# Gated linear attention and a routed expert layer on one core: steps moved between the places of a slot

## The chip, the cores and the metric

The kernel runs on one core of one Trainium2 chip. A core has five engines that each run their own instructions in order and wait for one another through semaphores: TensorE (PE in the profile; its weight loads are a row of their own, PEld), VectorE (DVE), ScalarE (ACT), GpSimd (POOL) and SyncE (SP, which issues most transfers). The metric is the device time of one execution in microseconds; lower is better.

## The reference

Four sequences of 768 tokens with 8 heads of 48 go through a gated linear attention; its output, 3072 tokens of 384 numbers, goes through a layer of 8 experts, of which each token uses one.

```python
for t in range(S):                        # attention: S = 768, per sequence and head
    state = alpha[:, :, t, :, None] * state + np.einsum('bhd,bhe->bhde', k[:, :, t], v[:, :, t])
    y[:, :, t] = np.einsum('bhd,bhde->bhe', q[:, :, t], state)
...
for s in range(S):                        # experts: x is the attention's output
    fresh_e = int(np.argmax(logits[b, s]))
    if s == 0 or local_gate[b, s] < 0.5:
        e = fresh_e
    else:
        e = prev_e if prev_e >= 0 else fresh_e
    prev_e = e
    ...
    h = np.maximum(x[b, s] @ w1[e], 0.0)  # 384 -> 1024
    out[b, s] = p[e] * (h @ w2[e])        # 1024 -> 384
```

`logits` is the token times `w_gate`, `p` its softmax, and `local_gate` a sigmoid of the token times `w_local`. Which expert a token uses can depend on the tokens before it, so it is known only once the attention has reached it.

## The kernel before

**Attention in slots.** The 3072 tokens are 24 blocks of 128, taken in turn from the four sequences. The main loop has 26 slots `i`. In slot `i` stand, in program order: GpSimd's `one_a(i+2)`, which sets one column of ones in the loaded decay factors `a`; `scan2(i+1)` (VectorE's backward scan `sf`, then GpSimd's product of it with `k`, both in the tile `x`); `flush()`; `kt(i)` (TensorE transposes `k` into `kp`, ScalarE copies that to `kk`); `copies(i-1)` and `state(i-1)` (ScalarE copies the state to `sb`, VectorE makes the next one); `pm(i)` (TensorE's products `pe`, masked by VectorE to `pq`); three prepared steps from the list `made`; the first place; `scan1(i+2)` (VectorE's scan `A` and a reciprocal, GpSimd's product of `A` with `q`); loads of block `i+3`; `xt(i-2)` (transposes `xp` for the routing); `ym(i-1)` (TensorE's output products `y`, from `pq` and from `sb`; ScalarE copies it to `XR` and sends it to `xd` in memory); the weights' step; the second place; `um(i)` (TensorE's products `up`, which VectorE adds into the state `st`; in slots 0 to 3 GpSimd first clears that state); the third place. From `pinned[0] = True` on, each engine keeps this order.

**Places.** A place is one call of `other()` (lines 622 to 636). It first runs `flush()`, which issues the VectorE steps put off in the list `later`; then it takes one step of each routing that is under way; and then, while `work[0]` is empty, two products of zeros on TensorE (`dense(DN)`, lines 293 to 295: 128x256 into `h2`, whose result nobody reads). Once `work[0]` is set it takes steps of the early experts instead, one for each place, in the second and third places only as long as blocks come in (`other(i >= NB)`), and no zeros.

**Routing.** After every four blocks `route(g)` is put on the list `steps` in slot 4g+5, ahead of its second place. It is a generator: what stands between two `yield` is done in one place. Its chain is `lg` (logits), `lt`, `kr` (VectorE, seven small steps), an empty place, `rp`, `em`, `rb`, `oi`, `ex`, `pw`, `ps` (seven or eight small VectorE steps), `vo` and `on` over four places (in the last routing one), and `lp`, which VectorE adds into the lists `acc`: 16 places, in the last routing 13. All its results on TensorE (`lg`, `lt`, `rp`, `rb`, `pw`, `lp`) use one PSUM buffer, the tag `rt`.

**Early experts.** The third routing (`g = 2`) ends by making the first lists `idx` and setting `work[0] = early()`. This generator gathers the rows of expert 0 (two indirect transfers on GpSimd's queue, one a place), waits four places, transposes them (`trans`, tiles `tp`, `xh`, `xl`; `tp` shares the PSUM tag `tr` with `kp` and `xp`), and then multiplies: a piece of `gemm1` is nine products into `h` with ScalarE's `hh` and VectorE's `hl` behind it, a piece of `gemm2` six products into `yp`. Three jobs run this way (256 rows of expert 0, 256 and 224 of expert 1); what is left of the eight experts follows behind the loop as a dense stretch of products.

**Weights.** `Weights.steps()` (lines 145 to 160) brings in one expert in seven steps: a load of the raw tile on SP's queue some steps ahead, ScalarE's rounding copy (`w1h`, `w2h`), and a subtraction for the rest (`w1l`, `w2l`), which for the early experts is put off through `later` and runs on VectorE at the next `flush()`. Expert 0 takes one step a slot in slots 5 to 11, ahead of the second place (lines 717 to 721); expert 1's seven steps are taken between the pieces of the first job's `gemm2`.

**The start.** Ahead of the loop GpSimd clears the tiles `vt`, `sb` and `oh`, sets the constants `one`, `m5`, `c0`, `c1` and `trif`, and then `one_a(0)`; TensorE runs 32 products of zeros. `made` holds twelve prepared steps, three a slot, from `fill` over `acc`, `off`, `ioa` and `iob` to `vals`.

Of the kernel before, what the change touches and what calls it, by code (L numbers as in the profile page):

```python
# [66 lines left out]
def gla_moe(ctx, tc, akq, vw, vn, wg, w1, w2, cst, tok, out):  # L67
# [188 lines left out]
    with ExitStack() as ac, ExitStack() as aa:  # L256
# [16 lines left out]
        for j in range(2):  # L273
            sb = ap.tile([R, 2, 2, CW], F32, bufs=1, name=f"sb{j}")
            g_.memset(sb[0:64], 0.0)
            g_.memset(sb[64:112, :, 1, :], 0.0)
            SBs.append(sb)
            oh = ap.tile([128, E, G + 1], F32, bufs=1, name=f"oh{j}")
            g_.memset(oh, 0.0)
            OHs.append(oh)  # L280
# [38 lines left out]
        def scan1(i):  # L319

            d = blk[i]
            x, a = d["x"], d["a"]
            A = ap.tile([R, SW], F32, tag="A", bufs=3, name=f"A_{i}")
            v_.tensor_tensor_scan(A, a[:, 0:SW], z1, 0.0, ALU.mult, ALU.add)
            d["end"] = A[:, 2 * C + 1:SW:2 * (C + 1)]
            v_.reciprocal(z2[0:R, 2 * C + 1:SW:2 * (C + 1)], d["end"])
            q2 = x[:, BW:].rearrange("p (s t) -> p s t", t=C)
            g_.tensor_tensor(q2, q2, A.rearrange("p (s t) -> p s t", t=C + 1)[:, :, 1:], ALU.mult)
            d["k"] = x[:, 0:BW].rearrange("p (h t) -> p h t", h=HP)
            d["q"] = x[:, BW:2 * BW].rearrange("p (h t) -> p h t", h=HP)  # L330

# [100 lines left out]
        def route(g):  # L432
# [36 lines left out]
            yield  # L469
# [66 lines left out]
            if end:  # L536
                v_.tensor_tensor(on, iob.unsqueeze(1).broadcast_to([128, n, TS]),
                                 rr.unsqueeze(2).broadcast_to([128, n, TS]), ALU.is_equal)
            else:
                for j in range(n):  # L540
                    s_.activation(on[:, j], iob, AF.Abs, bias=rr[:, j:j + 1], scale=-1.0)
                    s_.activation(on[:, j], on[:, j], AF.Relu, bias=one[:, 0:1], scale=-float(TS))
                    if j < n - 1:
                        yield
# [17 lines left out]
        def early():  # L562
# [10 lines left out]
            for _ in range(4):  # L573
                yield False
# [47 lines left out]
        def other(pieces=True):  # L622

            flush()
            for r in list(steps):
                if next(r, 0) == 0:
                    steps.remove(r)
            if work[0] is None:
                if DN:
                    dense(DN)  # L630
            else:
                if last and drained[0]:
                    last[0].ht, last[0].yt = HL, YL
                for done in work[0] if pieces else ():
                    if done or steps or not drained[0]:
                        break

# [9 lines left out]
        g_.memset(one, 1.0)  # L647
        g_.memset(m5, 1.0)
        g_.memset(m5[:, :, 0], 0.0)
        for e in range(E):  # L650
            g_.memset(c0[:, e:e + 1], float(e * RS - 1))
            g_.memset(c1[:, e:e + 1], float(e * RS - 1 + (C1 if e in EARLY else 0)))
        g_.tensor_copy(trif, cc("tri"))
        g_.memset(trif[0:64, 64:128], 1.0)
        g_.memset(trif[64:128, 0:64], 0.0)
# [4 lines left out]
        made = [  # L660
            lambda: g_.memset(fill, 0.0),
# [14 lines left out]
            lambda: g_.tensor_copy(vals[:, :, 2], tk[:, 1:2 * NB:2]),  # L676
        ]
        one_a(0)
        scan1(0)
        scan2(0)  # L680
        one_a(1)
        scan1(1)
        wsteps = iter(())
        for i in range(NB + 2):
# [14 lines left out]
            for _ in range(min(3, len(made))):  # L699
# [20 lines left out]
            elif i > W0 + 2:  # L720
                next(wsteps, None)
            if i == T1:
                begin(EARLY[1], v_)
            other()
            if i < NB:
                um(i)
# [214 lines left out]
```

## Time and profile before

| | |
|---|---|
| time, median of 3 runs | 482.89 us (481.34 to 493.2) |
| profiled execution | 484.0 us, of which the span is 482.2 |
| instructions | 10873 |
| mean granted TensorE clock | 0.961 |
| products of zeros (`h<-dz`) | 142, 35.0 us busy |
| routing's gathers and stores of rows | 32 and 32, about 1.0 us of GpSimd each |
| bytes moved | 66.01 MB, mean 137 GB/s |

A busy TensorE need not be at its peak, since products are pipelined; `TENSOR_TENSOR_SCAN` is VectorE's running sum along a row. In a timeline row stand start and duration in us, engine, line, operation, `out<-in` by the program's names, the shape, and in brackets how long the engine was idle just before and what ended that. Since one helper records every operation, all have line 81; the tile's name tells them apart. Consecutive instructions overlap by some tens of ns, so that the distance of two starts is a better price than a duration.

### The profile page before, as it was taken

The page shows a single profiled execution, that of the slowest core. Times are in us where ns is not written, and L with a number is a line of the kernel's source. Part 1 is how long each engine was busy: PE and PEld are TensorE (multiplying, and loading weights), DVE is VectorE, ACT ScalarE, POOL GpSimd, SP SyncE. Part 2 cuts the span into 40 slices and gives each one's busy share as a digit, 9 for nine tenths or more (in the row PEclk, how much of TensorE's full clock was granted, in tenths as well). Part 3 has the DMA queues.
Part 4 walks back from the last instruction along what each step waited for, and adds up shares of the span by engine and source line. Part 5 has one row for each costly group of instructions (what it writes and reads, how often), then busy time and mean ns, then how long its engine had stood idle before and what let it go on. Part 6 is the DMA issues. An engine that isn't in the chain of part 4 may idle for free.

```text
span 482.2 us, 10873 instructions
## 1 busy us (share of the span) xinstructions
PE 437.9 (91%) x4443; PEld 391.5 (81%) x4443; DVE 257.3 (53%) x485; ACT 194.1 (40%) x390; POOL 186.7 (39%) x207
## 2 busy tenths in 40 slices
PE   5999898999997978698989999999999999999990
PEld 5777776878875877597878998998989989989990
DVE  4778999898997235722274445244254252342310
ACT  1345656565756436321354324335144233242210
POOL 6654326364556000261053642724732503504201
PEclk9799999999998899888899999999999999999997
DMA  8789767596661102660075554444351542531100
GB/s 217 199 260 252 222 187 201 164 292 167 189 208 50 51 17 71 180 186 27 1 224 188 134 181 138 124 131 123 114 175 57 158 130 65 174 98 39 50 3 27
DMA packets 26710, 66.01 MB, mean 137 GB/s; under 512 B 4384, under 2 KB 10677, under 8 KB 26658
## 3 DMA queue, kind: packets, MB, share of 16 engines
q1 hardware_dynamic: 18672, 49.65, 36.3%
q0 software_dynamic: 3840, 10.62, 6.9%
q10 hardware_dynamic: 4146, 5.03, 3.1%
q8 instruction: 35, 0.57, 0.5%
q14 instruction: 17, 0.14, 0.1%
HBM read 55.84 MB, written 10.62 MB: 138 GB/s over the span
## 4 chain that ended last, share of the span: by engine, by line
PE 53%; issue 11%; DVE 9%; ACT 3%; POOL 2%; POOLq 0%; DVEq 0%; ACTq 0%
PE h L81 24%; PE yp L81 20%; PE y L81 3%; PE tp L81 2%; DVE A L81 2%; POOL out L81 1%; PE up L81 1%; DVE st L81 1%; DVE sf L81 1%; DVE pq L81 1%; ACT hh L81 1%; POOL w1l_0b L81 1%; PE pe L81 1%; DVE xl L81 1%; PE lp L81 1%
## 5 line engine op out<-in xcount | busy, mean ns | idle before, releaser
L81 DVE SCALAR_TENSOR_TENSOR hl<-h,hh 128x480 fp32r<-128x480 f32 (+2 forms) x80 | 43.9, 556 | 77.2 <-ACT hh L81 76.9
L81 ACT ACTIVATE hh<-h 128x480 fp32r<-128x480 f32 (+2 forms) x80 | 38.7, 490 | 82.4 <-PE h L81 82.3
L81 POOL DMA_INDIRECT out<-yo,idx x32 | 32.5, 1017 | 80.5 <-DVE yo L81 78.0
L81 POOL DMA_INDIRECT xg<-xd,idx x32 | 32.6, 1018 | 61.0 <-PE tp L81 52.9
L81 DVE TENSOR_SCALAR yo<-yp,acc 128x384 f32<-128x384 f32 (+1 forms) x32 | 19.6, 616 | 61.1 <-PE yp L81 61.0
L81 POOL TENSOR_TENSOR x<-x,sf 112x512 f32<-112x512 f32 x24 | 29.0, 1209 | 42.5 <-DVE sf L81 42.5
L81 POOL TENSOR_TENSOR x<-x,A 112x512 f32<-112x512 f32 x24 | 31.8, 1327 | 29.0 <-DVE A L81 6.6
L81 DVE TENSOR_TENSOR_SCAN A<-a,z 112x520 f32<-112x520 f32 x24 | 34.5, 1437 | 5.6 <-POOL a L81 5.6
L81 PE MATMUL h<-dz 128*128 128x256 f32 x142 | 35.0, 354 | 2.1 <-DVE z L81 2.1
L81 DVE TENSOR_TENSOR_SCAN sf<-a,z 112x520 f32<-112x520 f32 x24 | 33.8, 1408 | 0.1
L81 ACT COPY sb<-st 48x384 f32<-48x384 f32 x48 | 24.5, 510 | 11.5 <-DVE st L81 10.9
L81 PEld LDWEIGHTS h<-dz 128*128 128x128 f32 x142 | 23.8, 224 | 6.5 <-DVE z L81 2.1
L81 PEld LDWEIGHTS y<-vt,pq 64*64 64x64 f32 x768 | 24.9, 138 | 4.0 <-issue 3.8
L81 PE MATMUL y<-vt,pq 64*64 64x48 f32 x768 | 27.9, 224 | 0.0
L81 PE MATMUL y<-sb,x 112*64 112x96 f32 x384 | 21.8, 258 | 4.3 <-ACT sb L81 4.2
L81 PE MATMUL up<-vt,kk 128*48 128x96 f32 (+1 forms) x384 | 23.1, 267 | 0.0
L81 PEld LDWEIGHTS y<-sb,x 112*64 112x64 f32 x384 | 17.2, 140 | 6.2 <-ACT sb L81 5.2
L81 PEld LDWEIGHTS up<-vt,kk 128*48 128x48 f32 (+1 forms) x384 | 18.3, 140 | 3.4 <-issue 1.0
L81 ACT COPY kk<-kp 128x448 f32<-128x448 f32 x24 | 12.8, 531 | 20.7 <-PE kp L81 20.6
L81 PE MATMUL h<-xh,w1h_1a 128*128 128x256 f32 (+1 forms) x48 | 16.4, 342 | 3.9 <-DVE hl L81 2.7
L81 ACT COPY XR<-y 128x384 f32<-128x384 f32 x24 | 11.5, 479 | 20.1 <-PE y L81 20.1
L81 ACT CAST xh<-tp 128x384 fp32r<-128x384 f32 (+1 forms) x32 | 14.0, 462 | 13.9 <-PE tp L81 13.6
(247 smaller groups left out, 1234.8 us busy)
## 6 DMA issues: line engine op xcount, KB each, us to landing
x<-akq SPq DMA_DIRECT2D x24, 448.0 KB, 5.6
a<-akq SPq DMA_DIRECT2D x24, 227.9 KB, 4.5
vt<-vn SPq DMA_DIRECT2D x24, 192.0 KB, 2.7
xd<-XR ACTq DMA_DIRECT2D x24, 192.0 KB, 4.8
rw_0a<-w SPq DMA_DIRECT2D x3, 512.0 KB, 4.9
rw_0a<-w SPq DMA_DIRECT2D x4, 384.0 KB, 4.2
rw_1a<-w SPq DMA_DIRECT2D x3, 512.0 KB, 5.9
rw_1a<-w SPq DMA_DIRECT2D x4, 384.0 KB, 3.5
```

Of the source, the lines that this page charges most:

```text
L81: r = f(*a, **k)
```

## The change

Four parts are changed at once.

- The start: the clearing of the second `sb`, of `oh`, and the constants `one`, `m5` and `trif` go from the start to the head of `made`. `c0` is no longer written by eight small GpSimd steps but computed from `ioa` by two VectorE steps at the end of `made`, and `c1` by a copy of it and two small steps. A slot takes five prepared steps instead of three. The product of `A` with `q` for block 0 (`scale_q(0)`) goes behind that of `sf` with `k`.
- The weights' step of slots 5 to 11 goes behind the second place and ahead of `um(i)`, so that its put-off subtraction runs in the third place, behind the addition into `st`.
- The routing loses its empty place, and `on` takes two places instead of four: 13 places, in the last routing 12. `early()` waits two places instead of four.
- Zeros are also issued while `work[0]` is set, as long as no job has begun its first `gemm1` (`last` is empty), in each place in which no transposes or products of the early experts are issued.

```diff
@@ -272,12 +272,11 @@
             VTs.append(vt)
         for j in range(2):
             sb = ap.tile([R, 2, 2, CW], F32, bufs=1, name=f"sb{j}")
-            g_.memset(sb[0:64], 0.0)
-            g_.memset(sb[64:112, :, 1, :], 0.0)
+            if j == 0:
+                g_.memset(sb[0:64], 0.0)
+                g_.memset(sb[64:112, :, 1, :], 0.0)
             SBs.append(sb)
-            oh = ap.tile([128, E, G + 1], F32, bufs=1, name=f"oh{j}")
-            g_.memset(oh, 0.0)
-            OHs.append(oh)
+            OHs.append(ap.tile([128, E, G + 1], F32, bufs=1, name=f"oh{j}"))
 
         st = {"c": c0}
         sts = [ap.tile([R, 3, HP, D], F32, tag="st", bufs=G + 1, name=f"st_{i}") for i in range(G)]
@@ -324,10 +323,15 @@
             v_.tensor_tensor_scan(A, a[:, 0:SW], z1, 0.0, ALU.mult, ALU.add)
             d["end"] = A[:, 2 * C + 1:SW:2 * (C + 1)]
             v_.reciprocal(z2[0:R, 2 * C + 1:SW:2 * (C + 1)], d["end"])
-            q2 = x[:, BW:].rearrange("p (s t) -> p s t", t=C)
-            g_.tensor_tensor(q2, q2, A.rearrange("p (s t) -> p s t", t=C + 1)[:, :, 1:], ALU.mult)
+            d["A"] = A
+            if i:
+                scale_q(i)
             d["k"] = x[:, 0:BW].rearrange("p (h t) -> p h t", h=HP)
             d["q"] = x[:, BW:2 * BW].rearrange("p (h t) -> p h t", h=HP)
+
+        def scale_q(i):
+            q2 = blk[i]["x"][:, BW:].rearrange("p (s t) -> p s t", t=C)
+            g_.tensor_tensor(q2, q2, blk[i].pop("A").rearrange("p (s t) -> p s t", t=C + 1)[:, :, 1:], ALU.mult)
 
         def one_a(i):
             a = blk[i]["a"]
@@ -466,7 +470,6 @@
             v_.scalar_tensor_tensor(m2, kr[:, 1, :, 0], 16.0, m2, ALU.mult, ALU.add)
             v_.tensor_tensor(kr[:, 0], ge, m2.unsqueeze(2).broadcast_to([128, n, 8]), ALU.is_equal)
             yield
-            yield
 
             rp = pp.tile([8 * n, 2, 128], F32, tag=RT, name=f"rp_{g}")
             for j in range(2):
@@ -540,7 +543,7 @@
                 for j in range(n):
                     s_.activation(on[:, j], iob, AF.Abs, bias=rr[:, j:j + 1], scale=-1.0)
                     s_.activation(on[:, j], on[:, j], AF.Relu, bias=one[:, 0:1], scale=-float(TS))
-                    if j < n - 1:
+                    if j == 1:
                         yield
             yield
 
@@ -570,8 +573,8 @@
                 j.load_list(0)
             for _ in jobs[0].gather():
                 yield False
-            for _ in range(4):
-                yield False
+            yield False
+            yield False
             for _ in jobs[0].trans():
                 yield True
             for n, j in enumerate(jobs):
@@ -625,15 +628,15 @@
             for r in list(steps):
                 if next(r, 0) == 0:
                     steps.remove(r)
-            if work[0] is None:
-                if DN:
-                    dense(DN)
-            else:
+            done = False
+            if work[0] is not None:
                 if last and drained[0]:
                     last[0].ht, last[0].yt = HL, YL
                 for done in work[0] if pieces else ():
                     if done or steps or not drained[0]:
                         break
+            if not done and not drained[0] and (work[0] is None or not last):
+                dense(DN)
 
         work, drained = [None], [False]
         for i in range(3):
@@ -644,20 +647,21 @@
                 nc.scalar.dma_start(cs, cst)
                 nc.scalar.dma_start(tk, tok)
                 nc.scalar.dma_start(wgs, wg[:, :, 0:32])
-        g_.memset(one, 1.0)
-        g_.memset(m5, 1.0)
-        g_.memset(m5[:, :, 0], 0.0)
-        for e in range(E):
-            g_.memset(c0[:, e:e + 1], float(e * RS - 1))
-            g_.memset(c1[:, e:e + 1], float(e * RS - 1 + (C1 if e in EARLY else 0)))
-        g_.tensor_copy(trif, cc("tri"))
-        g_.memset(trif[0:64, 64:128], 1.0)
-        g_.memset(trif[64:128, 0:64], 0.0)
         nc.scalar.dma_start(xd[0:1], z2[127:128, 0:DM])
         first_v(0)
         pinned[0] = True
         dense(DN0)
         made = [
+            lambda: g_.memset(SBs[1][0:64], 0.0),
+            lambda: g_.memset(SBs[1][64:112, :, 1, :], 0.0),
+            lambda: g_.memset(one, 1.0),
+            lambda: g_.memset(OHs[0], 0.0),
+            lambda: g_.memset(OHs[1], 0.0),
+            lambda: g_.memset(m5, 1.0),
+            lambda: g_.memset(m5[:, :, 0], 0.0),
+            lambda: g_.tensor_copy(trif, cc("tri")),
+            lambda: g_.memset(trif[0:64, 64:128], 1.0),
+            lambda: g_.memset(trif[64:128, 0:64], 0.0),
             lambda: g_.memset(fill, 0.0),
             lambda: g_.tensor_copy(fill.bitcast(I32)[:, 1:2], tk[0:SL, 2 * NB:]),
             lambda: g_.memset(acc, 0.0),
@@ -674,10 +678,16 @@
                                      tk[:, 0:2 * NB].rearrange("p (b j t) -> p t j b", b=G, t=2)[:, 0],
                                      -float(SENT), None, ALU.add),
             lambda: g_.tensor_copy(vals[:, :, 2], tk[:, 1:2 * NB:2]),
+            lambda: v_.tensor_scalar(c0, ioa[:, :, 0], WH, float(TS), ALU.subtract, ALU.mult),
+            lambda: v_.tensor_scalar(c0, c0, -1.0, None, ALU.add),
+            lambda: g_.tensor_copy(c1, c0),
+        ] + [
+            lambda e=e: g_.memset(c1[:, e:e + 1], float(e * RS - 1 + C1)) for e in EARLY
         ]
         one_a(0)
         scan1(0)
         scan2(0)
+        scale_q(0)
         one_a(1)
         scan1(1)
         wsteps = iter(())
@@ -696,7 +706,7 @@
                 pm(i)
             if i > NB:
                 drained[0] = True
-            for _ in range(min(3, len(made))):
+            for _ in range(min(5, len(made))):
                 made.pop(0)()
             other(i >= NB)
             if i + 2 < NB:
@@ -717,11 +727,11 @@
             if i == W0:
                 begin(EARLY[0], v_)
                 wsteps = EW[EARLY[0]].steps()
-            elif i > W0 + 2:
-                next(wsteps, None)
             if i == T1:
                 begin(EARLY[1], v_)
             other()
+            if i > W0 + 2:
+                next(wsteps, None)
             if i < NB:
                 um(i)
             other()
```

## The prediction

> **What bounds the kernel now.** I read the page first (engines, the 40 slices), then the windows view cut at the starts of the slots, then the timeline and the waits inside the slots that the change touches.
>
> ```profile
> PE 437.9 (91%) x4443; PEld 391.5 (81%) x4443; DVE 257.3 (53%) x485; ACT 194.1 (40%) x390; POOL 186.7 (39%) x207
> ...
> PEclk9799999999998899888899999999999999999997
> ```
>
> TensorE is busy for 91% of the span and at full clock in most slices, so only three things can go: its idle time, its time at a lower clock, and multiplications of zeros. Where those lie, the windows view tells. I cut it at the transposes `kp` of slots 0, 5, 12, 17, 21 and 23, at the last `lg`, and behind it. Columns: length, then busy time and instructions of TensorE, its weight load, VectorE, ScalarE and GpSimd, then the granted clock, the DMA share and GB/s.
>
> ```profile
> 11.25:40.63 29.38, 27.02 (x492) 22.60 (x493) 23.25 (x32) 12.23 (x25) 15.89 (x28) 0.89 0.85 240
> 40.63:88.96 48.33, 43.41 (x833) 36.27 (x832) 43.43 (x82) 29.74 (x66) 21.51 (x24) 0.96 0.68 196
> 88.96:119.94 30.98, 30.20 (x591) 25.48 (x590) 28.27 (x62) 18.64 (x45) 14.28 (x15) 1.00 0.77 226
> 119.94:142.53 22.59, 21.77 (x462) 18.20 (x461) 21.66 (x45) 15.17 (x37) 13.18 (x15) 1.00 0.73 214
> 142.53:163.21 20.68, 16.81 (x256) 13.82 (x257) 12.24 (x31) 10.14 (x26) 9.40 (x8) 0.83 0.19 54
> 163.21:180.97 17.76, 15.12 (x218) 13.22 (x216) 6.14 (x23) 7.70 (x19) 0.83 (x1) 1.00 0.07 24
> 180.97:203.94 22.97, 16.82 (x122) 14.60 (x121) 16.00 (x42) 11.08 (x24) 3.14 (x3) 0.96 0.44 127
> ...
> 262.00:420.00 158.00, 158.00 (x848) 146.29 (x847) 62.72 (x94) 56.92 (x90) 67.27 (x46) 1.00 0.43 129
> ```
>
> Slots 5 to 11 (second row) leave 4.9 us idle on TensorE and as much on VectorE: each waits for the other in turns. Slots 12 to 16 are bound by TensorE, with 0.8 us idle. From 142.5 to 203.9 TensorE idles 3.9, 2.6 and 6.2 us, and the clock drops. From 262 us on it is always busy; nothing there is touched, so what the change gains before stays gained.
>
> **The change part by part.** Costs are taken against the profiled execution: 484.0 us, of which 482.2 are the span. The median of the three runs is 482.89, 1.1 us less.
>
> *(a) GpSimd's constants and the start.* The first scan waits for `one_a(0)` on GpSimd, behind its constants.
>
> ```profile
> 3.34 1.20 POOL L81 MEMSET sb<- 64x768 f32 x2
> ...
> 6.20 0.11 POOL L81 MEMSET a<- 112x4 f32 x1
> 6.34 1.24 DVE L81 TENSOR_TENSOR_SCAN A<-a,z 112x520 f32<-112x520 f32 x1 [4.23 <-POOL a L81]
> ...
> 7.67 1.18 POOL L81 TENSOR_TENSOR x<-x,A 112x512 f32<-112x512 f32 x1 [1.36 <-DVE A L81]
> ...
> 7.83 2.11 DVE L81 TENSOR_TENSOR_SCAN sf<-a,z 112x520 f32<-112x520 f32 x1
> ...
> 11.28 1.24 DVE L81 TENSOR_TENSOR_SCAN A<-a,z 112x520 f32<-112x520 f32 x1 [1.33 <-POOL a L81]
> ...
> 36.56 0.56 DVE L81 TENSOR_TENSOR st<-up,st 112x384 f32<-112x384 f32 x1 [1.54 <-POOL st L81]
> ```
> ```profile
> cs<-cst ACTq DMA_DIRECT2D x1, 224.5 KB, 4.5
> ```
>
> What stands from 3.34 to 6.20 on GpSimd, 2.9 us, leaves the start. Then the load of `a` is late next: its landing has no row; `cs`, as large and issued at the same time (0.7 us), took 4.5, so about 5.2. The scan starts at 5.35 instead of 6.34. With the product for `q` moved back, the scan `sf` no longer runs beside it and takes 1.22 (row under (b)) instead of 2.11; but that product, 1.18, now stands between `k` and `one_a(1)`. The second scan: 5.35 + 1.24 for `A` + 0.25 to `sf` (as from 7.58 to 7.83) + 1.22 + 1.18 for each product + 0.23 for `one_a(1)` and two hand-overs = 10.65, against 11.28: -0.6 (bounds -1.0, and 0 if `a` lands only at 6.2). The 2.9 us come back on GpSimd in slots 0 and 1, all other prepared steps slide back by two slots, and three VectorE steps (`ioa`, `iob`) meet in slot 3. In slots 0 to 3 the step `st` waits for GpSimd (last row), so this is not free; but GpSimd waits for the scan `A` there too, which covers most. I take a fifth of 2.9, +0.6 (bounds 0 and +2.9). Sum of (a): 0.0.
>
> *(b) Weights' step behind the second place, slots 5 to 11.* ScalarE's rounding copy and VectorE's subtraction are the same instructions; the three loads of a step stay behind the same loads on SP's queue, as nothing else is issued there in between.
>
> ```profile
> DVE w1l_0a L81 <- ACT w1h_0a L81: 2.2, 3, 1.2
> DVE w2l_0a L81 <- ACT w2h_0a L81: 0.4, 1, 0.4
> ...
> DVE w2l_0a L81 <- ACT w2h_0a L81: 2.0, 1, 2.0
> ```
> ```profile
> 53.68 1.88 DVE L81 TENSOR_TENSOR w1l_0a<-rw_0a,w1h_0a 128x1024 fp32r<-128x1024 f32 x1 [0.31 <-ACT w1h_0a L81]
> 55.47 0.55 DVE L81 TENSOR_TENSOR st<-up,st 112x384 f32<-112x384 f32 x1
> 55.94 1.22 DVE L81 TENSOR_TENSOR_SCAN sf<-a,z 112x520 f32<-112x520 f32 x1
> ```
>
> VectorE waits 4.6 us in all for the rounding copies; the addition into the state `st`, ready since `up`, and the copies and products behind it wait along. After, `st` goes first: 0.47 us of each wait (55.47 to 55.94) is filled, some 1.6 over the four waits in slots 5 to 8, and 1.0 of the long one in slot 11, where the routing's steps stand ahead too. I take -2.6 (bounds 0, and -4.6 if all waits go). ScalarE's copy now stands behind the second place's small copies and just ahead of the next slot's `kk`; its idle time covers that, at 29.74 busy of 48.33.
>
> *(c) Routing in 13 places instead of 16 (the last in 12 instead of 13).* No instruction goes. But a routing starts every 12 places, in a slot's second place. Now the last step of one (`lp`, and VectorE's addition into `acc`) and the first of the next (`lg`) fall into the same place, and `lp` and `lg` share the one buffer `rt`. So TensorE stands at `lg` until `acc` is read, and `acc` stands behind the scan `A`. Behind `lg` are zeros and `up`, and for `up` wait `st` and the next scan. Before, slot 14 shows the same wait at `rp`, a place later and behind `up`:
>
> ```profile
> 98.60 1.36 PE L81 MATMUL lg<-xx,wgs 128*32 128x128 f32 x24
> ...
> 105.46 1.13 PE L81 MATMUL lp<-vo,on 128*128 128x96 f32 x8
> 106.37 0.48 PE L81 MATMUL h<-dz 128*128 128x256 f32 x2
> 106.78 0.88 PE L81 MATMUL up<-vt,kk 128*48 128x96 f32 x16
> 108.19 0.39 PE L81 MATMUL rp<-cs,kr 128*32 128x128 f32 x2 [0.53 <-DVE acc L81]
> ```
> ```profile
> 106.55 1.23 DVE L81 TENSOR_TENSOR_SCAN A<-a,z 112x520 f32<-112x520 f32 x1
> 107.82 0.18 DVE L81 RECIPROCAL z<-A 112x4 f32<-112x4 f32 x1
> 107.91 0.23 DVE L81 TENSOR_TENSOR acc<-acc,lp 128x96 f32<-128x96 f32 x1
> 108.06 0.55 DVE L81 TENSOR_TENSOR st<-up,st 112x384 f32<-112x384 f32 x1
> ```
>
> `lp` makes way at 106.37, `acc` is done at 108.14: 1.77 us idle, less the 0.53 that `rp` waits no more, is 1.2 a slot. Slots 9, 13 and 17 together: +3.6. Bounds: 0, if `acc` comes early, and +2.6 each, if VectorE is the bound: then it idles from 108.14 over `lg` (1.36), zeros (0.41, from 106.37 to 106.78) and `up` (0.88), that is +7.9. I take TensorE's value, since these slots are bound by it.
>
> *(d) Zeros up to the first early multiplication.* `early` is begun one slot sooner and has two steps less ahead of its first product, and takes two steps a slot: its first product moves from slot 22's third place to slot 20's. Zeros end with slot 18's first place now; after, they stand in five more: slot 18's other two, slot 19's first two, slot 20's first. That is 10 products more, 0.205 us each (106.37 to 106.78 for two), 2.1 us. VectorE is busy 21.66 of 22.59 us in slots 17 to 20 and hides a third: +1.5 (bounds 0 and +2.1). The two gathers of the first job are issued on GpSimd one slot sooner, between the same products for `k` and `q`; GpSimd, busy 13.18 of 22.59 us there, covers them, and without that the next `k` would come later by their issue.
>
> *(e) Four pieces of the first products two slots earlier.* They lengthen slots 20 to 24 by what they take, since TensorE has little idle time there, and leave the last routing. In it three of the seven weight steps, of this size, are then gone too, and one place:
>
> ```profile
> L81 DVE TENSOR_TENSOR w1l_1a<-rw_1a,w1h_1a 128x1024 fp32r<-128x1024 f32 x3 | 3.7, 1223 | 1.0 <-ACT w1h_1a L81 1.0
> ```
>
> The pieces move, their time stays; what can go is the 6.2 us that TensorE idles from 180.97 to 203.94 behind the chain of the routing's steps on VectorE. With 3.7 us less there, I take half: -3.1 (bounds 0 and -6.2).
>
> *(f) The clock.* Two stretches at half clock cost TensorE half their length.
>
> ```profile
> 149.96 0.49 PE L81 MATMUL tp<-cs,xg 128*128 128x128 f32 x3
> 152.31 0.57 PE L81 MATMUL kp<-cs,x 112*128 112x112 f32 x4 [1.86 <-issue]
> ```
> ```profile
> 151.68 0.53 DVE L81 TENSOR_TENSOR xl<-tp,xh 128x384 fp32r<-128x384 f32 x1
> ```
> ```profile
> 190.00:200.00 10.00, 5.41 (x33) 4.44 (x31) 8.34 (x24) 4.08 (x7) 1.56 (x2) 1.00 0.71 210
> ...
> 154.50:161.00 6.50, 6.50 (x67) 5.85 (x65) 1.16 (x7) 2.54 (x7) 1.49 (x2) 0.50 0.21 64
> 202.50:208.00 5.50, 4.78 (x23) 4.31 (x23) 1.68 (x6) 0.77 (x2) 4.04 (x4) 0.50 0.84 266
> ```
>
> The first (3.2 us lost) follows a gap at `kp(22)`: it shares its buffer with `tp`, and stands until VectorE's `xl` behind a scan has read that. The order stays, two slots earlier, with the same gap at `kp(20)`; the zeros are issued on both sides of it and not in it. So I let it come back: 0. The second (2.75 lost) follows 10 us in which TensorE was busy for 54%. With 3.1 us less idle time in (e) that share rises above 70%, and I let the stretch go: -2.7 (bounds 0 and, with the first, -6.0).
>
> [...]
>
> Sum: 0.0 - 2.6 + 3.6 + 1.5 - 3.1 - 2.7 = -3.3, that is 480.7 on the profiled execution and 479.6 on the median: **480 us**.
>
> **The rivals.** *Both cold stretches go*, as zeros keep TensorE busy up to the gap: -3.2 more, 477. For it: clock 1.00 in slots 12 to 20, which have zeros. Against: the gap stays.
>
> *The waits at `lg` are covered as well*, because the places, more evenly filled, bring `acc` before `lp` ends, and all 4.6 us of (b) go: -3.6 and -2.0 more, 471. Against: `acc` stands behind a scan in the program.
>
> *Hidden anyway*: the last routing's chain is no shorter, both cold stretches come back: 484.0 + 0.0 - 2.6 + 3.6 + 1.5 = 486.5. For it: VectorE's chain, busy 8.34 of 10 us, sets that stretch.
>
> *Slower*: the wait at `lg` is long enough to drop the clock. Each of slots 9, 13, 17 and 21 then costs VectorE's 2.6 and half of a 6.5 us stretch, 5.9 in all: 23.6 for four in place of 3.6, 484.0 - 3.3 + 20.0 = 500.7. It decides from 4.2 a slot on: without (c) the sum is -6.9, and 9.7 us more than nothing need 16.6 over four slots. For it: 1.86 us idle was enough at `kp(22)`. Against: slot 14's wait at `rp` left the clock at 1.00 in 88.96 to 119.94.
>
> **How the numbers follow.** Forecast 37% (own range 478 to 483), both stretches 22%, waits covered 15%, hidden anyway 20%, slower 6%. Two per cent, about what a measurement of this kernel can tell from no change, are 9.7 us: faster over that is the third case and a tail of the second, 20%; slower 6%; the rest 74%. The range leaves out the slower case and half of the 471: 470 to 488.
>
> **What would show it.** Right: the first scan starts near 5.4 us and `sf` takes 1.2; no VectorE wait for `w1h` over 0.7 in slots 5 to 8; TensorE idle before `lg` in slots 9, 13 and 17, released by `acc`; first products in slot 20; a gap at `kp(20)`; the last routing under 20 us with its end at full clock. Wrong: `lg` without a wait, zeros that lengthen nothing, or half clock in slots 9 to 17.

## The result, and the profile after

| | before | after |
|---|---|---|
| time, median of four runs | 486.42 us (481.34 to 493.2) | 506.79 us (505.52 to 508.19) |
| ratio, 95% interval | | 1.0512 [1.0456, 1.0569] |
| span of the profiled execution | 482.2 us | 504.6 us |
| mean granted TensorE clock | 0.961 | 0.925 |
| span times (1 - clock) | 18.8 us | 37.8 us |

The ratio leaves out the slower two of the four runs of the kernel before (489.95 and 493.2), and so is more than the quotient of the medians. The changed kernel is 5% slower, 19 us beyond the end of the range. The last row is an estimate of the time that the clock takes, as if TensorE were the bound all along: of the 22.4 us between the spans it makes up 19.0. It is rather too high: in `warm_gap` below this figure falls by 17.1 us and the span by 12.4.

The page of the changed kernel, the 40 slices: the clock's row has dips in the first half that were not there before.

```profile
PE   6799879979897988879798999999999999999990
...
PEclk9699976968959799889889999999999999999997
```

The windows view, cut at the starts of slots (columns as in the prediction): first the kernel before, slots 5 to 8, then 9, 13 and 17 alone, then slots 18 and 19 and the 18 us behind the last `lg`.

```profile
40.63:67.46 26.83, 24.77 (x470) 20.75 (x469) 24.08 (x45) 15.62 (x33) 9.96 (x13) 0.94 0.70 202
67.46:75.52 8.06, 6.72 (x137) 5.32 (x136) 7.60 (x15) 5.85 (x15) 4.20 (x5) 1.00 0.86 247
...
94.86:101.71 6.85, 6.65 (x136) 5.32 (x135) 6.61 (x15) 4.90 (x13) 3.67 (x4) 1.00 1.01 349
...
119.94:126.54 6.60, 6.25 (x136) 5.19 (x135) 6.01 (x16) 4.90 (x13) 4.28 (x5) 1.00 0.73 206
126.54:137.09 10.55, 10.44 (x221) 8.82 (x220) 10.31 (x20) 6.94 (x18) 6.50 (x9) 1.00 0.66 191
...
180.97:199.00 18.03, 14.02 (x104) 12.24 (x103) 12.03 (x34) 10.70 (x23) 1.05 (x1) 1.00 0.41 111
```

The same stretches of the changed kernel, with slot 20 added:

```profile
41.12:66.51 25.39, 23.19 (x470) 19.64 (x469) 24.10 (x44) 15.80 (x34) 10.38 (x16) 1.00 0.81 221
66.51:82.21 15.70, 12.16 (x144) 9.97 (x143) 9.26 (x19) 7.54 (x18) 5.60 (x6) 0.63 0.61 174
...
101.00:116.46 15.46, 12.16 (x145) 9.97 (x143) 7.91 (x18) 6.15 (x16) 4.55 (x6) 0.62 0.72 227
...
134.04:147.20 13.16, 11.02 (x145) 9.00 (x143) 7.08 (x17) 6.14 (x16) 6.18 (x9) 0.68 0.62 170
147.20:162.04 14.84, 12.01 (x223) 9.95 (x223) 13.08 (x30) 6.79 (x16) 6.38 (x7) 0.94 0.55 161
162.04:172.66 10.62, 10.05 (x121) 8.53 (x122) 6.85 (x14) 4.79 (x11) 3.81 (x5) 0.68 0.21 62
...
209.99:228.00 18.01, 14.46 (x95) 13.21 (x96) 12.44 (x35) 6.63 (x14) 2.04 (x2) 0.81 0.57 171
```

Slots 9, 13 and 17, in which one routing ends and the next begins, take 15.70, 15.46 and 13.16 us instead of 8.06, 6.85 and 6.60: +22.8 us, as much as the whole loss. TensorE has the same work in them but for the eight products of `lp`, which stood in the next slot before, and is busy almost twice as long, at a clock of 0.62 to 0.68. The rest cancels: the start and slots 0 to 8 -1.0, slots 10 to 12 and 14 to 16 -1.2, slot 18 to the last `lg` +8.4, and from the last `lg` to the end 294.6 us instead of 301.2, -6.6.

What happens inside, the timeline of the changed kernel, slot 13:

```profile
101.00 0.55 PE L81 MATMUL kp<-cs,x 112*128 112x112 f32 x4
...
101.61 1.06 DVE L81 TENSOR_TENSOR po<-ps,oh 128x32 f32<-128x32 f32 x1
...
103.33 0.16 DVE L81 SCALAR_TENSOR_TENSOR rr<-sl,pt 128x4 f32<-128x4 f32 x1
...
103.52 0.40 ACT L81 ACTIVATE on<-iob,rr 128x128 f32<-128x128 f32 x1 [2.60 <-DVE rr L81]
...
104.68 0.40 ACT L81 ACTIVATE on<-on,one 128x128 f32<-128x128 f32 x1
...
104.99 0.51 ACT L81 COPY kk<-kp 128x448 f32<-128x448 f32 x1
...
105.56 0.90 PE L81 MATMUL xp<-cs,XR 128*128 128x128 f32 x3 [2.95 <-ACT kk L81]
106.39 1.95 PE L81 MATMUL y<-vt,pq 64*64 64x48 f32 x32
...
112.11 1.51 PE L81 MATMUL lg<-xx,wgs 128*32 128x128 f32 x24 [0.35 <-DVE acc L81]
...
114.28 1.55 PE L81 MATMUL up<-vt,kk 128*48 128x96 f32 x16
...
115.86 0.56 DVE L81 TENSOR_TENSOR st<-up,st 112x384 f32<-112x384 f32 x1 [3.81 <-PE up L81]
```

Read it backwards from 105.56. `xp` shares its PSUM buffer with `kp` and needs the copy `kk` to be done; `kp` was there at 101.55, but ScalarE runs `kk` only at 104.99, behind the four steps of `on` that stand ahead of it in the program, and the first of these waits for VectorE's `rr` (idle for 2.60 us). TensorE idles 2.95 us, and from there on its rows are long: `up` takes 1.55 us where the prediction's row has 0.88, and VectorE has waited 3.81 us when it is done. The windows view at the edges of that stretch:

```profile
104.50:105.00 0.50, 0.00 (x0) 0.00 (x0) 0.50 (x1) 0.47 (x3) 0.14 (x2) 0.74 1.07 428
105.00:118.25 13.25, 12.35 (x140) 10.29 (x140) 5.48 (x9) 5.51 (x15) 3.08 (x4) 0.50 0.56 167
118.25:118.50 0.25, 0.25 (x11) 0.13 (x5) 0.00 (x0) 0.25 (x1) 0.25 (x1) 0.71 0.00 0
```

The clock falls at 104.74 (0.74 over half a microsecond is half clock for 0.26 of it), 2.1 us after TensorE ran dry, and comes back only at 118.39, although TensorE is busy for 12.35 of the 13.25 us in the middle row.

### The profile page after: what moved, and what is told of

Same layout as the page of the kernel before. It is cut to its first block, busy times and chain, and to the rows that moved or that the text cites. A ratio compares the mean times of both kernels' runs of the same rounds, so it can differ in the third digit from the quotient of the medians.

```text
span 504.6 us, 10881 instructions
## 1 busy us (share of the span) xinstructions
PE 454.3 (90%) x4453; PEld 405.1 (80%) x4453; DVE 258.3 (51%) x487; ACT 195.4 (39%) x390; POOL 181.6 (36%) x194
## 4 chain that ended last, share of the span: by engine, by line
PE 50%; issue 11%; DVE 5%; ACT 3%; DMA 2%; POOL 2%; POOLq 0%; ACTq 0%
PE h L81 21%; PE yp L81 19%; PE y L81 3%; DMA rw_4b<-w 2%; PE tp L81 1%; PE up L81 1%; POOL out L81 1%; PE pe L81 1%; ACT on L81 1%; PE lp L81 1%; PE xp L81 1%; DVE hl L81 1%; PE lg L81 1%; POOL w1l_0b L81 1%; PE kp L81 1%
## 5 line engine op out<-in xcount | busy, mean ns | idle before, releaser
L81 PE MATMUL h<-dz 128*128 128x256 f32 x152 | 38.4, 357 | 2.1 <-DVE z L81 2.1
L81 POOL TENSOR_TENSOR x<-x,A 112x512 f32<-112x512 f32 x24 | 28.5, 1187 | 32.1 <-PE rp L81 10.4
L81 DVE TENSOR_TENSOR_SCAN sf<-a,z 112x520 f32<-112x520 f32 x24 | 32.4, 1349 | 0.1
L81 PEld LDWEIGHTS h<-dz 128*128 128x128 f32 x152 | 25.8, 223 | 8.1 <-DVE z L81 2.1
L81 PEld LDWEIGHTS y<-vt,pq 64*64 64x64 f32 x768 | 27.4, 149 | 4.5 <-issue 4.5
L81 PE MATMUL y<-vt,pq 64*64 64x48 f32 x768 | 30.5, 235 | 0.0
L81 DVE TENSOR_TENSOR st<-up,st 112x384 f32<-112x384 f32 (+1 forms) x24 | 12.4, 517 | 31.4 <-PE up L81 25.2
L81 PE MATMUL y<-sb,x 112*64 112x96 f32 x384 | 24.6, 278 | 0.3 <-ACT sb L81 0.3
L81 PE MATMUL h<-xh,w1h_1a 128*128 128x256 f32 (+1 forms) x48 | 15.8, 330 | 6.4 <-DVE hl L81 5.9
L81 PEld LDWEIGHTS y<-sb,x 112*64 112x64 f32 x384 | 19.6, 154 | 1.8 <-ACT sb L81 0.4
L81 PE MATMUL kp<-cs,x 112*128 112x112 f32 x96 | 14.9, 282 | 6.8 <-POOL x L81 3.9
```

What stands on the lines that cost most here:

```text
L81: r = f(*a, **k)
```

## Experiments

Each kernel is told by its edit; "before" and "after" are the two kernels above. Ratios are to the kernel before on the same chip; where two changed kernels are compared, it is by these ratios. Slots and waits are read from one profiled execution of each kernel.

### Which part of the change

`routing_as_before` is the changed kernel with the 16 places of the routing; `routing_alone` the kernel before with the routing of 13 places and nothing else; `start_and_weights` the kernel before with parts (a) and (b) alone.

```diff
@@ route(g), the two edits that routing_as_before undoes and routing_alone makes
             v_.tensor_tensor(kr[:, 0], ge, ..., ALU.is_equal)
             yield
-            yield
...
-                    if j < n - 1:
+                    if j == 1:
                         yield
```

> The changed kernel with the routing in 16 places again (the empty place and one pair of `on` a place); all else as changed, early() with two empty places too. Theories A and B alike: slots 9, 13 and 17 as in the kernel before (8.1, 6.9, 6.6 us), time 476 to 484: the other parts together gain 0 to 7 us. If instead the other parts cost something, the time is over 486.

> The kernel before with the routing's three places taken out and nothing else changed. Theories A and B: it alone makes the loss, 500 to 510; slots 9, 13 and 17 at 12 to 16 us. If the loss needs the other parts too (zeros, weights' step, constants): under 492.

> The kernel before with the change's start and constants, and the weights' step behind the second place; routing, early() and zeros as before. By the prediction's terms (a) and (b), 0.0 and -2.6: slot 12 starts 2 to 3 us sooner than in the kernel before (88.96), and the time is 2 to 3 us under its time. If what was gained by slot 12 is given back later: within 1 us.

Measured: 485.2 us, ratio 1.0049 [1.0015, 1.0083]; 513.63 us, 1.0579 [1.0527, 1.0632]; 485.61 us, 0.9996 [0.9957, 1.0034]. The routing alone makes all of the loss, a little more than the 500 to 510 expected, and without it slots 9, 13 and 17 take 6.63, 6.59 and 6.59 us. The 485.2 of `routing_as_before` lies between its two ranges: the other parts together gain nothing. Parts (a) and (b) bring slot 12 forward by 2.2 us (86.80 against 88.96), which does not arrive at the end.

### Which step of the routing

`on_later` takes all of `on` one place later, behind `kk`; `lp_later` takes `lp` one place later; `empty_back` and `on_back` each undo one of the two edits above. All are on the changed kernel.

```diff
@@ on_later
             else:
+                yield
                 for j in range(n):
                     s_.activation(on[:, j], iob, AF.Abs, ...)
...
-                    if j == 1:
-                        yield
@@ lp_later
             yield
+            yield
 
             lp = pp.tile([128, 3 * E * NS], F32, tag=RT, name=f"lp_{g}")
```

> The changed kernel, but the four steps `on` of a routing stand one place later, in the first place of slots 9, 13 and 17, behind the copy `kk` on ScalarE; `vo` stays, the routing has 13 places as before, and `lp` and `lg` still share a place. Theory A (the four `on`, waiting for VectorE's `rr`, hold up `kk` behind them on ScalarE, so that `xp` waits for the buffer `tr` and the clock falls): no gap over 1 us before `xp` in slots 9, 13 and 17, clock 1.00 there, these slots 8 to 10 us instead of 15.7, 15.5 and 13.2, time 484 to 490. Theory B (the wait of `lg` for `acc` in the shared buffer `rt`): these slots stay over 12 us, time over 500.

> The changed kernel, but `lp` one place later (14 places), so that `lg` no longer stands behind it; `on` stays ahead of `kk`. Theory A: the gap of about 3 us before `xp` and the half clock in slots 9, 13 and 17 stay, these slots over 12 us, time 500 to 508. Theory B: `lg` does not wait, these slots 7 to 9 us, time 483 to 490.

> The changed kernel with only the empty place back (14 places): `ps` falls into a third place again, behind `st`, the first four steps `on` behind `kk`, and `lp` one place behind `lg`. Theory C (both A and B hold, each by itself enough to drop the clock, and both hang on where `ps`, `on` and `lp` fall in the slot): no gap over 1.2 us in slots 9, 13 and 17, these slots 6.5 to 8.5 us, time 482 to 489. If the four `on` in one place are what costs: these slots over 10 us, time over 493.

> The changed kernel with only the four places of `on` back (15 places), the empty place still out: `ps` stays in the second place, two steps `on` ahead of `kk`, `lp` one slot later. Theory C: `kk` still waits for `rr`, a gap of about 2.1 us before `xp` (3.0 less two steps `on`), these slots 7 to 13 us, time 486 to 500, worse than the kernel with only the empty place back by 3 or more. If the number of places of `on` is what counts: as good as or better than that.

Measured: 499.99 us, 1.0284 [1.0227, 1.0340]; 500.97 us, 1.0309 [1.0258, 1.0361]; 494.34 us, 1.0155 [1.0109, 1.0202]; 496.49 us, 1.0251 [1.0187, 1.0315]. Every one gives back some and none all of it. What each theory expected of its own cure was missed (A of `on_later`, B of `lp_later`), and so was the 482 to 489 for `empty_back`; what A expected of `lp_later` came. `on_back` lies in its range of 486 to 500, but is not told apart from `empty_back`, than which it was to be worse by 3 us.

In each, waits of 1.1 to 3.2 us stay or take the place of the one removed. In `lp_later` and `on_back` the gap ahead of `xp` stays: in slots 9, 13 and 17 it is 3.21, 2.95 and 1.74 us in the one, 2.48, 2.22 and 1.07 us in the other. In `on_later` `y` waits 1.53 and 1.27 us for `sb` in slots 9 and 13, and in slot 13 `lp` for each piece of `on`. In `empty_back` `lg` waits 2.07 us in slot 9 for the copy `xx`, which now stands behind `on` on ScalarE, but there is no gap ahead of `xp`. So it is the empty place that kept `on` behind `kk`: without it the gap is there with two steps of `on` a place (`on_back`) as with four, which only lengthen it.

### Is it the wait, or the clock behind it

`warm_gap` leaves every wait and fills TensorE's idle time with products of zeros.

```diff
             other(i >= NB)
+            if i in (9, 13, 17):
+                dense(14)
             if i + 2 < NB:
                 scan1(i + 2)
```

> The changed kernel with 14 more products of zeros (2.9 us at full clock) behind the first place of slots 9, 13 and 17, where TensorE stands 3.19, 2.95 and 2.5 us at the transposes `xp`. The wait itself stays. Theory D (the wait costs its own 3 us, and what doubles it is the half clock behind it): the clock stays at 0.9 or more in slots 9, 13 and 17, each takes 10.5 to 12.5 us instead of 15.7, 15.5 and 13.2, and the time falls to 490-498. Rival (the slots are long because of the chain of waits, the clock is a companion): the slots stay at 13 or more and the time at 503-512.

Measured: 492.59 us, 1.0189 [1.0097, 1.0281]. Adding 42 products made the changed kernel some 14 us faster, in the range that theory D expected; its clock of 0.9 or more came in two of the three slots. The windows view of slots 9, 13 and 17:

```profile
65.90:80.67 14.77, 12.86 (x158) 10.83 (x157) 9.30 (x19) 7.54 (x18) 5.62 (x6) 0.71 0.60 181
...
99.27:110.09 10.82, 9.19 (x158) 7.83 (x157) 7.61 (x17) 5.90 (x16) 4.57 (x6) 1.00 0.97 292
126.84:136.50 9.66, 9.19 (x158) 7.82 (x157) 6.77 (x16) 5.90 (x16) 5.43 (x8) 1.00 0.63 171
```

In slots 13 and 17 the clock holds, and they are 4.6 and 3.5 us shorter with the same wait; in slot 9, 1.56 us of the gap were left uncovered and the clock fell as before. So the clock is a cause of its own, 3.5 to 4.6 us a slot, beside 3 to 4 us of waiting (10.82 against 6.85, 9.66 against 6.60).

### Which waits

`on_gpsimd` and `on_vector` make `on` by comparisons (`is_equal`) on another engine, in 13 places; `on_vector_lg` also gives `lg` a buffer of its own. `on_gpsimd_tp` is told of below.

```diff
@@ on_vector
-                for j in range(n):
-                    s_.activation(on[:, j], iob, AF.Abs, ...)
...
+            v_.tensor_tensor(on, iob..., rr..., ALU.is_equal)
+            if not end:
+                yield
@@ on_vector_lg, besides
-            lg = pp.tile([128, 128], F32, tag=RT, name=f"lg_{g}")
+            lg = pp.tile([128, 128], F32, tag="yp" if g < NBB - 1 else RT, name=f"lg_{g}")
```

> The changed kernel, with `on` made by GpSimd (four comparisons, two places) instead of eight steps of ScalarE; 13 places as before. Theory C (the copies `kk` and `xx` stand behind `on` on ScalarE): no gap over 1 us ahead of `xp` in slots 9, 13 and 17, those slots take 7 to 9 us, and the time is 485-492. Rival E (VectorE's steps `ps` to `oa` in the second place hold up `st`, `sb` and the products whatever ScalarE does): gaps of 2 us move to `y` or `lp`, the slots stay at 11 to 14 and the time at 496-503.

> The changed kernel, with `on` in one VectorE step (0.68 us, as in the last routing) in place of eight steps of ScalarE; 13 places. Theory C: no gap over 1 us ahead of `xp`; slots 9, 13 and 17 take 7 to 9 us at a clock of 0.9 or more, and the time is 484-492. Theory E: the wait moves to `y` or `lp`, at 1.3 us or more, the clock falls all the same, the slots take 10 to 14 and the time is 494-503.

> on_vector, with `lg` in the idle buffer `yp` instead of the one that it shares with `lp` (but for the last routing). If the wait of `lg` for `acc` (2.12 us in slot 13) drops the clock: slots 9, 13 and 17 take 7 to 8.5 us at full clock instead of 13.5, 12.3 and 11.5, and the time is 478-486. If the wait of `y` for `sb` (1.28 us, ahead of it) is enough: the slots lose only the 2.1 to 2.4 us of the wait, 9.5 to 11, and the time is 488-492.

Measured: 502.77 us, 1.0411 [1.0309, 1.0512]; 496.44 us, 1.0246 [1.0182, 1.0310]; 486.93 us, 1.0048 [1.0003, 1.0092]. In `on_gpsimd` the gap at `xp` is gone, but a pair of GpSimd's comparisons takes 2.11 us and `lp` waits for them, 1.13 and 1.96 us in slot 9: a miss for theory C, while the time is in the range of E and the slots, 13.2 to 15.8 us, are mostly above it. `on_vector` came in the time and the slots that E expected. `kk` comes at once there, and what is left shows in the timeline of slot 13:

```profile
103.97 0.88 PE L81 MATMUL y<-sb,x 112*64 112x96 f32 x16 [1.28 <-ACT sb L81]
104.78 1.13 PE L81 MATMUL lp<-vo,on 128*128 128x96 f32 x8
108.03 1.51 PE L81 MATMUL lg<-xx,wgs 128*32 128x128 f32 x24 [2.12 <-DVE acc L81]
109.47 0.80 PE L81 MATMUL h<-dz 128*128 128x256 f32 x2
```

That is the wait of the prediction's step (c). Around it the windows view has the clock fall:

```profile
107.00:108.00 1.00, 0.00 (x0) 0.00 (x0) 0.94 (x3) 0.00 (x0) 0.24 (x1) 1.00 1.04 254
108.00:109.00 1.00, 0.97 (x20) 0.96 (x24) 0.00 (x0) 0.00 (x0) 0.97 (x2) 0.54 1.06 226
```

In slot 9 of `on_vector` it is another wait: there the clock fell at 73.94 us, before TensorE ran dry ahead of `lg` at 74.70, and behind a wait of 1.53 us of `y` for `sb`.

With a buffer for `lg` the ratio drops by 0.020, some 10 us for three slots, and the time, 486.93 us, lies between the two ranges expected. `all_cures` below has the same routing; its slots 9, 13 and 17:

```profile
66.24:78.18 11.94, 10.18 (x145) 8.43 (x144) 9.79 (x20) 4.70 (x10) 6.22 (x6) 0.72 0.75 229
96.43:105.22 8.79, 7.35 (x144) 6.14 (x143) 8.55 (x19) 3.22 (x8) 4.87 (x5) 1.00 0.98 300
122.13:129.50 7.37, 6.68 (x140) 5.61 (x139) 7.20 (x16) 3.19 (x7) 3.82 (x5) 1.00 0.75 199
```

So both answers hold, each in its place: in slots 13 and 17 it was the wait at `lg` that dropped the clock, which now stays at 1.00; in slot 9 the wait of `y` for `sb` is enough (0.72).

| slot | before | after | `on` off ScalarE (`on_vector`) | `lg` apart too (`all_cures`) |
|---|---|---|---|---|
| 9 | 8.06 | 15.70 | 13.51 | 11.94 |
| 13 | 6.85 | 15.46 | 12.33 | 8.79 |
| 17 | 6.60 | 13.16 | 11.54 | 7.37 |
| sum | 21.51 | 44.32 | 37.38 | 28.10 |

So of 22.8 us, with the cures taken in this order, 6.9 go with `kk` no longer behind `on`, 9.3 with `lg` no longer behind `acc`, and 6.6 stay, with the wait of `y` for `sb` (1.26 us in slot 13, 1.54 in slot 9), that is for VectorE, whose steps `ps` to `oa` now stand ahead of `st`.

### What the other parts are worth

Here the first early job's transposes `tp` get the idle buffer `yp`, so that `kp` need not wait for `xl`. `tp_own_buffer` is `routing_as_before` with that; `on_gpsimd_tp` is `on_gpsimd` with it; `tp_weights` is `start_and_weights` with it (16 places, four places of waiting in `early()`, zeros as before). `tp_early` has two places of waiting and is else `tp_weights`, `tp_zeros` has the zeros of the change, `tp_alone` is the kernel before with the buffer only, and `all_cures` is `tp_weights` with the routing of `on_vector_lg`.

```diff
-                tp = self.ps.tile([128, 3, m], F32, tag="tp" if self.pb[0] else "tr", ...)
+                tp = self.ps.tile([128, 3, m], F32, tag="tp" if self.pb[0] else self.tt, ...)
...
             for j in jobs[:2]:
                 j.load_list(0)
+            jobs[0].tt = "yp"
```

> The kernel with the routing as before (485.2 us), but the first job's transposes `tp` use the PSUM buffer of `yp`, which is idle then, instead of sharing `tr` with `kp`. Theory D (the gap of 3.8 us at `kp` of slot 21, behind VectorE's `xl`, drops the clock for slots 21 and 22): no gap there, clock 1.00, slots 20 to 22 together 21 to 25 us instead of 30.1, time 477 to 481. If the gap is hidden by VectorE, which is late anyway: over 483.

> The kernel on_gpsimd, and the first early job's transposes `tp` in the buffer `yp` instead of the one of `kp`. Theory C: 5 us less than on_gpsimd, from slots 20 to 22, that is 480-487, no clock below 0.9 from slot 12 to slot 22. Rival E: also 3 to 6 us less than on_gpsimd, but above 490.

> The kernel before with the start and the weights' step as changed, and `tp` in the buffer `yp`; 16 places, four places of waiting in the early generator and no more zeros than before. If the clock's first cold stretch in the kernel before (3.2 us lost behind the gap of 1.86 us at the transposes `kp` of slot 22) is caused by that gap alone: 480-483, no clock below 0.9 in slots 21 to 23. If the zeros and the earlier start of the first products carry part of what tp_own_buffer gained: 484-487.

> tp_weights, with two places of waiting ahead of the first early job instead of four, as in the change; zeros as before. If the earlier first products take cover from the last routing (TensorE idles more there and its clock falls): 2 to 5 us over tp_weights, clock under 0.9 in the 24 us behind the last `lg`. If the zeros did it: within 1.5 us of tp_weights, clock 1.00 there.

> tp_weights, with zeros up to the first early multiplication as in the change; four places of waiting. If the zeros lengthen the slots before the first products: 2 to 4 us over tp_weights, all of it by slot 23, clock 1.00 behind the last `lg`. If the earlier first products did it: within 1.5 us of tp_weights.

> The kernel before with `tp` in the buffer `yp` and nothing else. If the start and the weights' step are worth their 2.2 us of slot 12 once the clock holds: 2 to 3 us over tp_weights. If they are given back: within 1 us of it. If the buffer's gain hangs on them: 5 us or more over it.

> on_vector_lg, with `tp` in the buffer `yp`, four places of waiting ahead of the early job and the zeros as before: tp_weights with the routing of the change, its three waits cured. If 13 places are worth what the early start of the chain suggests: at or under tp_weights, ratio 0.975 to 0.985 to before. If the steps of VectorE in the second place cost the slots more than the shorter routing gives: 0.985 to 1.0.

| kernel | us | ratio, 95% interval | span | clock |
|---|---|---|---|---|
| tp_own_buffer | 482.95 | 0.9957 [0.9916, 0.9999] | 480.0 | 0.961 |
| on_gpsimd_tp | 502.6 | 1.0405 [1.0316, 1.0494] | 500.6 | 0.933 |
| tp_weights | 473.49 | 0.9824 [0.9733, 0.9915] | 471.1 | 0.978 |
| tp_early | 484.42 | 0.9997 [0.9952, 1.0043] | 482.9 | 0.951 |
| tp_zeros | 482.0 | 0.9926 [0.9870, 0.9982] | 476.4 | 0.971 |
| tp_alone | 482.78 | 0.9981 [0.9937, 1.0026] | 482.3 | 0.964 |
| all_cures | 489.0 | 1.0093 [1.0043, 1.0144] | 487.4 | 0.952 |

`tp_weights` is the fastest of all, 1.8% under the kernel before and below what was expected of it. Neither of its halves does that, the buffer alone (`tp_alone`, 0.9981, the third of the answers expected) or the start and the weights' step alone (0.9996); why both together do stays open. The kernels with the earlier first products or the buffer alone are slower than it, beyond both intervals; `tp_zeros` is not told apart from it. `tp_early` is some 8 us over `tp_weights`, more than the 2 to 5 expected. `tp_own_buffer` took 22.5 us for slots 20 to 22 at full clock, as expected, and missed its 477 to 481 all the same. `on_gpsimd_tp` gained nothing, against what was expected: slots 19 and 20 became 5.5 us shorter, and slot 21 with 14.2 us 3.5 longer. `all_cures` missed both of its ranges: even with two of its three waits cured (that of `y` for `sb` stays) the routing of 13 places is slower than that of 16. The windows view shows where the earlier products lose, behind slot 23; first `tp_early`, from the start of slot 23 on:

```profile
159.58:177.31 17.73, 15.08 (x215) 13.15 (x214) 6.14 (x23) 7.51 (x18) 0.83 (x1) 1.00 0.07 24
177.31:201.00 23.69, 16.52 (x108) 14.66 (x108) 14.80 (x38) 10.40 (x22) 2.50 (x2) 0.84 0.49 145
201.00:216.00 15.00, 13.09 (x85) 12.08 (x84) 3.30 (x11) 2.30 (x6) 9.99 (x10) 0.91 0.43 119
```

and `tp_weights`:

```profile
155.62:173.38 17.76, 15.11 (x218) 13.22 (x216) 6.14 (x23) 7.70 (x19) 0.83 (x1) 1.00 0.07 25
173.38:197.00 23.62, 17.35 (x130) 15.32 (x130) 16.33 (x44) 11.10 (x24) 3.52 (x4) 1.00 0.45 126
197.00:212.00 15.00, 14.07 (x99) 13.86 (x98) 3.59 (x8) 2.69 (x7) 9.62 (x10) 1.00 0.54 165
```

I read it so: pieces that are done earlier are missing as cover beside the last routing. In the same 24 us TensorE gets 108 products done instead of 130, and its clock is 0.84 instead of 1.00; which of the two brings the other was not tried.

## Why the prediction was wrong

The step that failed is (c), the routing in 13 places: +3.6 us with an upper bound of +7.9, measured +22.8. It failed in three ways.

1. *"No instruction goes"* counted the places as free. What they did was to keep ScalarE's queue open. The empty place held `rr`, and so `on`, behind the next slot's `kk`; without it the wait for `rr` stands ahead of `kk`, and four steps of `on` in one place make it longer. I looked for what is late next on TensorE and VectorE, not on ScalarE, although the two questions to a wait, who is queued behind it and who waits for that, lead from `on` over `kk` to `xp` in two steps. 6.9 us go with `on` off ScalarE.
2. The wait of `lg` for `acc` was named with its place and its mechanism, and it is real: 2.41 us in slot 9 and 2.12 in slot 13 of `on_vector`, where I took 1.77. In the changed kernel the other wait hides it, 0.35 us. It was priced at its length alone.
3. Both ends of the range of (c) assumed the full clock. The rival "slower" had the clock, 5.9 us a slot and 500.7 in all, and was given 6%, because slot 14's wait at `rp` had left the clock at 1.00. That row was a wait of 0.53 us; the row that was nearest to 1.77, the gap of 1.86 at `kp(22)`, spoke for the rival. By the point that I gave myself, 4.2 us a slot, it is decided at 7.6. That its number came near 506.5, the profiled execution, is in part luck: it had the wait at `lg` as the cause, which is 0.35 us here, and four slots in place of three. `warm_gap` shows that the clock makes about half of it.

The other steps:

- (a) 0.0: right. The first scan starts at 5.34 (5.35 forecast), the second at 10.55 (10.65), `sf` takes 1.24, and slot 5 starts at 41.12 against 40.63, in `tp_weights` at 40.71.

```profile
5.34 1.24 DVE L81 TENSOR_TENSOR_SCAN A<-a,z 112x520 f32<-112x520 f32 x1 [3.24 <-POOL a L81]
...
6.83 1.24 DVE L81 TENSOR_TENSOR_SCAN sf<-a,z 112x520 f32<-112x520 f32 x1
```

- (b) -2.6: right in size. From slot 5 to slot 12 `tp_weights` takes 46.2 us (40.71 to 86.92), before 48.3: -2.1. At the end it is not to be seen in `start_and_weights`.
- (d) +1.5: right in size. `tp_zeros` starts slot 23 at 157.35, `tp_weights` at 155.62: +1.7, of which 0.3 stood there at slot 17 already; the changed kernel has the 152 products of zeros that were counted.
- (e) -3.1: wrong in sign with 16 places. `tp_early` is some 8 us over `tp_weights` (0.9997 against 0.9824). In the profiles 4.0 are there by slot 23, but 1.4 of these by the start of slot 17, up to which the two programs do the same. I let the pieces move at no cost and did not count that they were the cover of the last routing, as the question what is late next would have asked. In the changed kernel itself the part behind the last `lg` is 6.6 us shorter; the clock does not make it, as both kernels spend 13.7 us at half clock there, besides the last 7 us of the span. Whether (e) does or the shorter last routing was not tried.
- (f) the first stretch returned, as forecast, with a gap of 2.84 us at `kp(20)`, in slot 20 at a clock of 0.68. The second I let go (-2.7), and it stayed: 0.81 in the row 209.99:228.00.

```profile
161.41 0.53 DVE L81 TENSOR_TENSOR xl<-tp,xh 128x384 fp32r<-128x384 f32 x1
...
162.04 0.57 PE L81 MATMUL kp<-cs,x 112*128 112x112 f32 x4 [2.84 <-issue]
```

Of the rivals, "both cold stretches go" fell with the half clock behind that gap, "waits covered" with slots 9 to 17, and "hidden anyway" lacked the same 19 us of (c) as the forecast. That gap was 2.84 us long, and the clock fell at 162.77. What stays open: why `all_cures` loses to `tp_weights` beyond the 7.8 us of slots 9, 13 and 17 (28.10 against 20.3).

## What to carry to other kernels

A wait of TensorE is not priced by its length where a trace has the clock fall behind it: in slots 13 and 17 here the half clock cost 4.6 and 3.5 us (`warm_gap`) beside 3 to 4 us of waiting. Half of the cold time is an estimate of that, rather too high. Span times (1 - clock), read for each kernel, tells at once about how much of a difference it is: here 19.0 of 22.4 us, rather too high as well. A place without an instruction of its own, or a step spread over several, can be what keeps a queue free for the copies that the next engine waits for, as the empty place did here for `kk` (without it `xp` waits 2.95 us in slot 13), so go through every engine's queue at the new place. Work moved earlier is taken from somewhere: look at what it covered there.

## What the runs showed of the clock

The half-clock stretches come in few lengths. In slot 13 of the changed kernel it is 13.65 us (104.74 to 118.39), and in slot 9 the same, 70.61 to 84.26:

```profile
70.50:70.75 0.25, 0.00 (x0) 0.00 (x0) 0.25 (x2) 0.25 (x2) 0.25 (x1) 0.72 0.07 29
70.75:84.00 13.25, 12.34 (x140) 10.29 (x140) 7.02 (x10) 6.25 (x16) 3.19 (x5) 0.50 0.44 115
84.00:84.50 0.50, 0.50 (x12) 0.38 (x7) 0.50 (x3) 0.49 (x2) 0.23 (x1) 0.74 0.00 0
```

Worked out in the same way from windows of 0.25 us, the stretches of the changed kernel that lie wholly inside the span are 3.4, 6.8, 10.2 or 13.65 us long, multiples of 3.41, and those of the kernel before 3.4 or 6.8. In the two stretches of 13.65 us, four such units, the clock stayed at 0.50 although TensorE was busy for 93% of the time (rows 70.75:84.00 and 105.00:118.25); what decides the number of units stays open.

The falls lie on a grid of that unit. In the changed kernel the clock falls at 15.99, 70.61, 104.74, 138.88, 162.77, 210.56, 224.21 and 248.10 us, whole multiples of 3.413 us apart (the first and the last are 68 of them apart, 232.11 us); the falls of the kernel before, at 10.85, 58.64, 154.21, 202.00 and 225.89 us, and those read from windows of 0.25 us in `all_cures`, `on_vector`, `tp_alone`, `tp_early`, `tp_own_buffer`, `tp_weights`, `tp_zeros` and `warm_gap` lie on such a grid too, to 0.02 us, each time with another offset. In the unit of time ahead of each of the eight falls of the changed kernel TensorE was busy for 0.14 to 0.48 of it, and in no other at full clock between 7 and 262 us for less than 0.66; in the kernel before these shares are 0.33 to 0.56 and 0.61. Over these other profiles they overlap: a share of 0.63 was followed by a fall in `tp_weights` (13.82 to 17.24 us), one of 0.55 was not in `all_cures` (214.90 to 218.32 us), and what else decides there stays open. So in these traces the falls go with the idle part of one such unit more closely than with the length of a single wait. The waits of 1.26 and 1.28 us in slot 13 of `all_cures` (share 0.63) and `warm_gap` (0.67) were not followed by half clock. The waits of 1.54 us and 1.56 us in slot 9 of these two (0.55 and 0.54), 1.86 us before (0.56) and 2.95 us after (0.38) were followed by it. As the offset of the grid differs between executions, the same wait may cost its clock in one and not in the next; that is argued here, not tried.
